# Single row blocks as seven half products, side by side in the array

## The chip, the cores and the metric

One core of a Trainium2 chip. The metric is the device time of one execution in microseconds. Before the change three runs gave 1431.31 to 1433.48, median 1432.56. The engines are named as in the profile: PE is TensorE (PEld its weight loads), DVE VectorE, ACT ScalarE, POOL GpSimd, SP SyncE, whose queue issues DMAs.

## What is computed

Batch 8, 4224 tokens, 192 channels. First a causal convolution of 7 taps over the tokens, with one softmax of taps per head of 24 channels; its result is `x` below. Then:

```python
theta = x @ w_theta
zr, zi = x * cos(theta), x * sin(theta)
y = einsum('ts,bsd->btd', w_tok_r, zr) + einsum('ts,bsd->btd', w_tok_i, zi)
u = x + y
out = u + maximum(u @ w_ch, 0)
```

The two products with the 4224 x 4224 token matrices are nearly all of the work.

## The kernel before, in words

The 4224 tokens are 33 **chunks** of 128 source tokens (four stretches of 32 from four quarters of the sequence), and 33 **row blocks** of 128 output tokens. A chunk is loaded (`load_chunk`), convolved (`conv`, L212), transposed, multiplied with `w_theta` (`theta`), and leaves in SBUF its values `z`: cosine and sine parts for two halves of the columns, Z11, Z12, Z21, Z22, and sums of these, T1 to T4 (`sums`, L303; the combinations of a Strassen-Winograd scheme). It holds a place among 11 for 17 steps.

A **step** (class `Step`, L343) multiplies the 11 chunks then in SBUF (fewer near the ends of a round) with the weights of two row blocks, a pair; 17 steps make a round, and there are 58 steps, 0 to 57. As 33 is odd, one step in each round has a single row block: steps 6, 23, 40 and 57. Steps 6 and 23 have all 11 chunks and are not among the last.

In a pair step the 2 x 2 blocks (two row blocks by cosine and sine weights "11", "12", "21", "22"; two halves of the 1536 columns) are done with seven products instead of eight. `load_w` (L376) loads one of the two weight matrices for the step by four POOL DMAs into a tile `st` (two buffers); `turn` (L394) transposes a part of it in blocks of 32x32 on DVE into a tile `wt` (nine buffers); `wsum` (L402) makes the sums S1 to S4. `w_tasks` (L414) and `early_tasks` say when. These transposed parts and sums are called the step's forms. `runs` (L492) lists the seven runs, each over all chunks, 2 x 11 matmuls of 128x384; `give` (L482) then adds a finished accumulator of 128x768 (PSUM) into the row block's partial sums `pv` in SBUF: on DVE, but on ACT as a copy where it is the first visit in the first round. Such an addition or copy is called an eviction. A single step has four runs without the scheme (11·Z11, 11·T1, 12·Z21, 12·Z22 with two accumulators): 88 matmuls, four times 22, and four evictions.

The accumulators are tiles of two PSUM banks; `ypool` has two (tag "y") and `mmpool` two (tag "mm", `banks`), the latter used otherwise for convolution, transposes and channel products. A run that opens on a reused accumulator must wait until its eviction has read it.

Order: each engine's own work is issued in an order written out by hand (`pe`, `dve`, `act`, `pool`, L85 to L95 chain each instruction to the one before on its engine). `step_events` (L719) collects for each step tasks with a place from 0 to 7 (sevenths of the step's matmuls); `mix` (L587) issues those that are due ahead of each matmul. So a DVE task stands in DVE's queue between the evictions of the runs around its place, and an instruction that waits there holds all that are behind it. DMAs of the SP queue are placed by the framework's scheduler.

Partial sums go to DRAM (`part`) at a step's end and come back one round later (`load_rows`). Into some of the second round's row blocks the convolution's result is added: `load_x` (L457) loads the rows into `xr` (one buffer) by the SP queue, `add_x` (L465) adds them on POOL, not before the DVE instruction issued just ahead of it has ended (`paced`). The first such blocks are the two of step 24, so their additions lie in step 23.

Of the kernel before, what the change touches and what calls it, by code (L numbers as in the profile page):

```python
# [9 lines left out]
AT = mybir.ActivationFunctionType  # L10
ALU = mybir.AluOpType
F16 = mybir.dt.float16
# [4 lines left out]
def kernel(  # L17
# [23 lines left out]
    nc = tc.nc  # L41
# [3 lines left out]
    P = nc.NUM_PARTITIONS  # L45
    assert (B, D, P) == (8, 192, 128) and S % P == 0
    N = B * D
    HD = D // 2
    HN = N // 2
    NQ = 4  # L50
    Q = P // NQ
# [7 lines left out]
    BH = HN // 2  # L59
    NU = (NT + 1) // 2  # L60
    NW = 11
# [5 lines left out]
    start = [base[k % NW] + (NU + 1) * (k // NW) for k in range(NK)]  # L67
# [17 lines left out]
    def pe(ins):  # L85
        return in_order("pe", ins)

    def dve(ins):
        return in_order("dve", ins)

    def act(ins):
        return in_order("act", ins)
# [11 lines left out]
    wpool = ctx.enter_context(tc.tile_pool(name="wpool", bufs=2))  # L104
# [10 lines left out]
    part = [dram.tile([NT, P, N], F32, name=f"part{i}") for i in range(2)]  # L115

    def banks(name, dtype=F32):
        return mmpool.tile([P, 2, PC if dtype == F32 else 2 * PC], dtype,
                           name=name, tag="mm")
# [11 lines left out]
    def loose(name, dtype=F32):  # L131
        return ypool.tile([P, 2, PC if dtype == F32 else 2 * PC], dtype,
                          name=name, tag="y")
# [50 lines left out]
    Z11, T1, Z21, Z22, T2, T4, T3 = range(7)  # L184
    Z12 = T3

    class Chunk:
# [120 lines left out]
        def sum(self, o, a, b):  # L308
            z = self.z
            dve(nc.vector.tensor_tensor(  # L310
                out=z[:, o, :], in0=z[:, a, :], in1=z[:, b, :], op=ALU.subtract
            ))
# [30 lines left out]
    class Step:  # L343


        def __init__(self, t):
            self.t, self.u, self.ks = t, unit(t), active(t)
            self.n = len(self.ks)
            self.tbs = [tb for tb in (2 * self.u, 2 * self.u + 1) if tb < NT]
            self.pair = len(self.tbs) == 2  # L350
            self.first = t < NU
            self.final = t + NU >= NSTEP
            self.late = self.final and self.n < NW
            visits = [v for v in range(NU, NSTEP) if v % NU == t % NU]
            quiet = [v for v in visits if start[2 * NW - 1] < v <= 2 * NU]
            self.adds, self.ahead = [], []
            for i, tb in enumerate(self.tbs):
                known = self.known(tb)
                if t not in ([v for v in quiet if known < v - 1] or visits[-1:])[:1]:
                    continue  # L360
                if not self.late:
                    self.adds.append(i)
                else:
                    far = known <= start[2 * NW - 1]
                    self.ahead.append((i, 2 * NU - NW + 2 * (t % NU) if far else start[-1],
                                       (t // NU - 1 - far) % 2))
            self.plain = self.first and self.pair and self.n <= NP
            self.time = 0.324 * self.n * (8 if self.plain else 7 if self.pair else 5 if self.n <= 2 else 4)
            self.closing = False
            self.st, self.w, self.xr, self.ub, self.uT, self.pv = {}, {}, {}, {}, {}, []  # L370

# [4 lines left out]
        def load_w(self, m):  # L376

            w = (moe_w_tok_r, moe_w_tok_i)[m - 1]
            st = wpool.tile([P, 2, NQ, NW * Q], F16, name="st", tag="st", bufs=2)
            n, nb = self.n * Q, len(self.tbs)  # L380
            for a in range(NQ):
                t0 = token(self.ks[0], a)
                pool(nc.gpsimd.dma_start(  # L383
                    out=st[a * Q : (a + 1) * Q, 0:nb, :, 0:n]
                    .rearrange("i r bt s -> i (r bt) s"),
                    in_=w[self.tbs[0] * P : (self.tbs[0] + nb) * P, t0 : t0 + n]
                    .rearrange("(bt i) s -> i bt s", i=Q),
                ))
            self.st[m] = st
# [4 lines left out]
        def turn(self, name):  # L394
            self.w[name] = self.wtile()
            dve(nc.vector.transpose(  # L396
                self.w[name][:, 0 : self.n, :, :],
                self.st[int(name[1])][:, int(name[0]) - 1, :, 0 : self.n * Q]
                .rearrange("p bt (c j) -> p c bt j", j=Q),
            ))  # L400

        def wsum(self, name):  # L402
            a, b, op = {
                "S1": ("21", "22", ALU.add), "S2": ("S1", "11", ALU.subtract),
                "S3": ("11", "21", ALU.subtract), "S4": ("12", "S2", ALU.subtract),
            }[name]
            self.w[name] = self.wtile()
            dve(nc.vector.tensor_tensor(  # L408
                out=self.w[name][:, 0 : self.n, :, :],
                in0=self.w[a][:, 0 : self.n, :, :],  # L410
                in1=self.w[b][:, 0 : self.n, :, :], op=op,
            ))

        def w_tasks(self):  # L414

            if not self.pair:
                return [(0.25, lambda: self.turn("11")), (4.2, lambda: self.turn("12"))]
            if self.plain:
                return []
            if self.ahead_of_single():  # L420
                return [
                    (0.3, lambda: self.turn("22")), (1.1, lambda: self.wsum("S1")),
                    (1.9, lambda: self.wsum("S2")), (2.9, lambda: self.turn("12")),
                    (4.0, lambda: self.wsum("S4")),
                ]
            return [
                (0.25, lambda: self.turn("11")), (1.2, lambda: self.turn("21")),
                (2.05, lambda: self.wsum("S3")), (2.2, lambda: self.turn("22")),
                (3.05, lambda: self.wsum("S1")), (3.3, lambda: self.wsum("S2")),
                (4.2, lambda: self.turn("12")), (5.1, lambda: self.wsum("S4")),  # L430
            ]

        def ahead_of_single(self):
            return self.final and not steps[self.t - 1].pair and self.pair

        def early_tasks(self):

            return [
                (5.9, lambda: self.turn("11")), (7.0, lambda: self.turn("21")),
                (7.01, lambda: self.wsum("S3")),  # L440
            ]
# [110 lines left out]
        def mix_halves(self, events):  # L552
# [31 lines left out]
            for _, f in events:  # L584
                f()

        def mix(self, events):  # L587

            if self.n <= 2 and not self.first:
                yield from self.mix_halves(events)  # L590
                return
            items = list(self.products())
            events = sorted(events, key=lambda e: e[0])
            y = {}
            for j, (wn, zn, cn, c, opens, closes, to) in enumerate(items):
                if opens:
                    y[cn] = ypool.tile([P, 2, PC], F32, name="y", tag="y")
                while events and events[0][0] * len(items) <= 7 * j:
                    events.pop(0)[1]()
                k = self.ks[c]  # L600
                yield k
                for q in range(2):
                    pe(nc.tensor.matmul(  # L603
                        y[cn][:, q, 0:BH],
                        lhsT=self.w[wn][:, c, :, :].rearrange("p bt i -> p (bt i)"),
                        rhs=chunks[k].z[:, zn, q * BH : (q + 1) * BH],
                        start=opens, stop=closes,
                        skip_group_check=True,
                    ))
                if to:  # L610
                    self.give(y[cn], *to)
            for _, f in events:
                f()
            if not self.final:
                for i, tb in enumerate(self.tbs):
                    nc.sync.dma_start(
                        out=part[(self.t // NU) % 2][tb, :, :], in_=self.pv[i]
                    )

        def cast_half(self, i, h, gs, by_dve):  # L620

# [97 lines left out]
    def step_events(t):  # L719
# [13 lines left out]
        if t + 2 < NSTEP:  # L733
            nxt = steps[t + 2]
            if steps[t + 1].ahead_of_single():
                found.append((4.5, lambda: nxt.load_rows(True)))
            for m in (1, 2):
                at = 1.3 + 3 * (m - 1)
                if steps[t + 1].ahead_of_single():
                    at = (0.1, 3.1)[m - 1]  # L740
                found.append((at, lambda m=m: nxt.load_w(m)))
            if nxt.ahead_of_single():
                found += nxt.early_tasks()
        if t == NPS:
            found.append((5.5, lambda: chunks[EARLY].plain_sums()))
        if t == NPS + 1:
# [241 lines left out]
```

## Time and profile before

| | |
|---|---|
| profiled execution | 1430.95 us |
| its span | 1429.2 us |
| median of three runs | 1432.56 us |
| PE busy | 1408.4 us, 99% |
| DVE busy | 973.2 us, 68% |
| POOL busy | 435.3 us, 30% |
| ACT busy | 312.0 us, 22% |
| granted TensorE clock | 0.999 |
| mixing matmuls (L603) | 7652, 1278.2 us |

The profile shows one execution. A group's row gives the line, the engine, what is written from what, the shape and the count; then its busy time, the mean length of one in ns, and after the bar the idle time of its engine just before, with what ended it. A timeline's row gives start and length in us; instructions in succession are merged, their number at the end. Matmuls overlap in the pipeline: a row of 0.326 us stands for a pitch (start to start) of half that.

### The profile page before, as it was taken

How to read it: one execution, taken by the hardware profiler on the slowest of the kernel's cores; microseconds unless marked ns; L12 is line 12 of the kernel's file. 1: busy time of each engine (PE TensorE's matmuls, PEld its weight loads, DVE VectorE, ACT ScalarE, POOL GpSimd, SP SyncE). 2: the span in 40 equal slices, each digit the busy share in tenths (PEclk: the TensorE clock that was granted, in tenths of full speed). 3: DMA queues.
4: the chain of work that ended last, by engine and by line, in shares of the span. 5: the costliest groups of instructions: out<-in, count | busy, mean ns of one | idle time of the engine just before them, and what ended most of it. 6: DMA issues, size and time to landing. Idle time of an engine off the chain costs nothing.

```text
span 1429.2 us, 23781 instructions
## 1 busy us (share of the span) xinstructions
PE 1408.4 (99%) x9829; PEld 889.5 (62%) x9829; DVE 973.2 (68%) x1047; ACT 312.0 (22%) x377; POOL 435.3 (30%) x655
## 2 busy tenths in 40 slices
PE   8899999999999999999999999999999999999997
PEld 5566666666666666666666666666566666666665
DVE  6884654545458787766665657877777677767686
ACT  5951111011134253000000004435100110010134
POOL 8521221111323322532333343233324123213110
PEclk9999999999999999999999999999999999999999
DMA  9975765564699999898899889999999999999784
GB/s 190 250 174 111 148 146 109 121 134 95 160 227 221 244 217 257 197 262 173 237 229 235 226 157 244 230 200 245 272 206 211 215 210 215 203 200 198 167 219 134
DMA packets 272046, 282.00 MB, mean 197 GB/s; under 512 B 106688, under 2 KB 240192, under 8 KB 271936
## 3 DMA queue, kind: packets, MB, share of 16 engines
q0 software_dynamic: 162464, 92.15, 49.0%
q1 hardware_dynamic: 71840, 178.88, 35.4%
q10 hardware_dynamic: 37632, 9.44, 4.3%
q8 instruction: 77, 1.26, 0.4%
q14 instruction: 33, 0.27, 0.1%
HBM read 245.49 MB, written 108.13 MB: 247 GB/s over the span
## 4 chain that ended last, share of the span: by engine, by line
PE 88%; DMA 5%; DVE 4%; ACT 1%; issue 1%; POOL 1%; SPq 0%; DVEq 0%; ACTq 0%; POOLq 0%
PE y L603 80%; PE v L150 5%; DMA st<-in_moe_w_tok_i_dram 2%; DMA st<-in_moe_w_tok_r_dram 1%; PE tp L174 1%; DMA xw<-in_x_dram 1%; PE pc L220 1%; DVE wt L396 1%; DVE pv L490 1%; ACT z L295 1%; POOL st L383 1%; DVE z L310 0%; DVE z L301 0%; DMA xs<-z 0%; DVE pv L652 0%
## 5 line engine op out<-in xcount | busy, mean ns | idle before, releaser
L603 PE MATMUL y<-z,wt 128*128 128x384 f16 x7652 | 1278.2, 326 | 2.1 <-DVE pv L490 1.0
L603 PEld LDWEIGHTS <-wt 128*128 128x128 f16 x7652 | 741.9, 98 | 477.2 <-issue 3.6
L490 DVE TENSOR_TENSOR pv<-y,pv 128x768 f32<-128x768 f32 x315 | 300.8, 955 | 320.5 <-PE y L603 274.9
L396 DVE STREAM_TRANSPOSE wt<-st 128x1408 f16<-128x1408 f16 (+7 forms) x224 | 327.7, 1466 | 44.2 <-PE y L603 36.2
L383 POOL DMA_DIRECT2D st<-in_moe_w_tok_r_dram x232 | 132.7, 578 | 457.9 <-DVE wt L396 450.9
L383 POOL DMA_DIRECT2D st<-in_moe_w_tok_i_dram x232 | 132.7, 579 | 402.6 <-DVE wt L396 390.3
L408 DVE TENSOR_TENSOR wt<-wt 128x1408 f16<-128x1408 f16 (+6 forms) x208 | 173.6, 835 | 41.8 <-PE y L603 39.4
L160 ACT ACTIVATE z<-pc 128x768 f16<-128x768 f32 (+1 forms) x62 | 47.5, 803 | 385.4 <-PE pc L220 381.1
L160 ACT ACTIVATE ub<-pv 128x768 f16<-128x768 f32 (+1 forms) x66 | 51.5, 821 | 338.7 <-DVE pv L490 336.9
L488 ACT ACTIVATE pv<-y 128x768 f32<-128x768 f32 x66 | 53.7, 814 | 278.5 <-PE y L603 278.5
L150 PEld LDWEIGHTS <-uT 128*128 128x128 f16 x1056 | 90.5, 98 | 22.9 <-issue 5.6
L468 POOL TENSOR_TENSOR pv<-pv,xr 128x1536 f32<-128x1536 f32 x24 | 74.5, 3104 | 66.1 <-issue 26.8
L207 POOL DMA_DIRECT2D xw<-in_x_dram x132 | 76.4, 585 | 28.8 <-DMA st<-in_moe_w_tok_r_dram 7.1
L652 DVE SCALAR_TENSOR_TENSOR pv<-v,pv 128x768 f32<-128x768 f32 (+1 forms) x67 | 63.0, 942 | 25.2 <-PE v L150 24.7
L310 DVE TENSOR_TENSOR z<-z 128x768 f16<-128x768 f16 x132 | 71.2, 553 | 2.3
L295 ACT ACTIVATE z<-v,half_pi 128x768 f16<-128x768 f32 x66 | 59.6, 903 | 56.2 <-PE v L150 55.5
L160 ACT ACTIVATE uT<-tp 128x1536 f16<-128x1536 f16 (+1 forms) x47 | 56.7, 1208 | 47.7 <-PE tp L174 47.7
L301 DVE TENSOR_TENSOR z<-z 128x1536 f16<-128x1536 f16 (+1 forms) x68 | 60.6, 926 | 5.1 <-ACT z L295 5.1
L150 PE MATMUL v<-wth,uT 128*128 128x192 f16 x528 | 54.4, 246 | 2.7 <-ACT z L295 2.1
L150 PE MATMUL v<-wch,uT 128*128 128x192 f16 x528 | 54.4, 246 | 0.8 <-DVE pv L652 0.5
L295 ACT ACTIVATE z<-v 128x768 f16<-128x768 f32 x66 | 53.2, 807 | 0.0
L220 PE MATMUL pc<-xw,bands 96*64 96x192 f16 x512 | 30.1, 250 | 4.1 <-DMA st<-in_moe_w_tok_r_dram 2.2
(48 smaller groups left out, 152.0 us busy)
## 6 DMA issues: line engine op xcount, KB each, us to landing
part<-pv SPq DMA_DIRECT2D x79, 768.0 KB, 4.3
pv<-part SPq DMA_DIRECT2D x79, 768.0 KB, 6.3
out_dram<-pv SPq DMA_DIRECT2D x65, 384.0 KB, 4.3
st<-in_moe_w_tok_r_dram POOLq DMA_DIRECT2D x136, 176.0 KB, 5.9
st<-in_moe_w_tok_i_dram POOLq DMA_DIRECT2D x136, 176.0 KB, 5.2
xs<-z SPq DMA_DIRECT2D x132, 96.0 KB, 5.2
xw<-in_x_dram POOLq DMA_DIRECT2D x121, 96.0 KB, 6.0
xr<-xs SPq DMA_DIRECT2D x24, 384.0 KB, 4.1
```

Of the source, the lines that this page charges most:

```text
L150: pe(nc.tensor.matmul(v[:, k, b * D : (b + 1) * D], lhsT=tT[:, 3 * k + b + i, :], rhs=w[:, 2 * b + i, :], start=(i == 0), stop=(i == 1),))
L160: act(nc.scalar.activation(out=out, in_=in_, func=AT.Copy))
L207: nc.gpsimd.dma_start(out=self.xw[lo : lo + n, h, :, :], in_=x[:, t0 : t0 + n, :].rearrange("b s d -> s b d"),)
L295: act(nc.scalar.activation(**args))
L310: dve(nc.vector.tensor_tensor(out=z[:, o, :], in0=z[:, a, :], in1=z[:, b, :], op=ALU.subtract))
L383: pool(nc.gpsimd.dma_start(out=st[a * Q : (a + 1) * Q, 0:nb, :, 0:n] .rearrange("i r bt s -> i (r bt) s"), in_=w[self.tbs[0] * P : (self.t ...
L396: dve(nc.vector.transpose(self.w[name][:, 0 : self.n, :, :], self.st[int(name[1])][:, int(name[0]) - 1, :, 0 : self.n * Q] .rearrange("p b ...
L408: dve(nc.vector.tensor_tensor(out=self.w[name][:, 0 : self.n, :, :], in0=self.w[a][:, 0 : self.n, :, :], in1=self.w[b][:, 0 : self.n, :, : ...
L468: ins = pool(nc.gpsimd.tensor_tensor(out=self.pv[i], in0=self.pv[i], in1=self.xr[i], op=ALU.add))
L490: dve(nc.vector.tensor_tensor(out=o, in0=yv, in1=o, op=ALU.add))
L603: pe(nc.tensor.matmul(y[cn][:, q, 0:BH], lhsT=self.w[wn][:, c, :, :].rearrange("p bt i -> p (bt i)"), rhs=chunks[k].z[:, zn, q * BH : (q + ...
L652: dve(nc.vector.scalar_tensor_tensor(out=ub[:, ks, :], in0=v[:, ks, :], scalar=0.0, in1=ub[:, ks, :], op0=ALU.max, op1=ALU.add,))
```

## The change

For steps 6 and 23 (`halves`) the single row block is cut into two halves of 64 rows, which take the part of the two row blocks in the seven-product scheme: 11 and 21 are the halves of the transposed cosine weights, 12 and 22 those of the sine weights. Each product has 64 output rows and 384 columns at a time, so two of them are placed side by side in the array, one in its columns 0 to 63 and one in 64 to 127, with accumulators of their own. Four slots: (11·Z11, S1·T1), (S2·T2, S4·Z22), (S3·T3, 12·Z21), and 22·T4 with six chunks on one side and five on the other. Within a slot all chunks are done for one half of the columns, then for the other, and each of the four accumulators is evicted (64 partitions by 384) before the next slot uses it again. The second side's accumulators come from `mmpool`.

The sums S1 to S4 of a single step are four DVE operations of 128 x 704. Both weight matrices of a single step go into one `st` tile, issued together, which leaves the other buffer for the next pair's first matrix, loaded one step earlier than before. The forms of the pair step behind a single step (7 and 24) are made during three steps instead of one: their "11" and "21" (for step 7 also S3, "22" and S1) in the step before the single one, the others within the single step, most of them at its end. The second weight load of the step after that (8 and 25) is moved from place 4.3 to 7.1 of the single step.

In the engines' queues: DVE gets "11" and "21" of step 24 into step 22, where "12" of step 23 stood and behind it; POOL has the two additions `add_x` of step 24 directly behind each other, then the weight load of step 25, which stood between them; SP has the load of `xr` for step 25's first addition ahead of the store of step 23's partial sums.

```diff
+            self.halves = not self.pair and self.n == NW and not self.final
...
         def load_w(self, m):
+            joint = self.halves and m == 2
+            if joint:
+                st = self.st[1]
+            else:
+                st = wpool.tile([P, 2, NQ, NW * Q], F16, name="st", tag="st", bufs=2)
...
+        def half(self, name):
+            tile, i = {
+                "11": ("11", 0), "21": ("11", 1), "12": ("12", 0), "22": ("12", 1),
+                "S1": ("S1", 0), "S2": ("S1", 1), "S3": ("S3", 0), "S4": ("S3", 1),
+            }[name]
+            return self.w[tile][:, :, 2 * i : 2 * i + 2, :]
...
         def w_tasks(self):
+            if self.halves:
+                return [(0.25, lambda: self.turn("11")), (1.2, lambda: self.turn("12")),
+                        (2.2, self.half_sums)]
             if not self.pair:
                 return [(0.25, lambda: self.turn("11")), (4.2, lambda: self.turn("12"))]
+            if self.behind_halves():
+                if steps[self.t - 1].first:
+                    return [(4.0, lambda: self.wsum("S2")), (7.0, lambda: self.turn("12")),
+                            (7.01, lambda: self.wsum("S4"))]
+                return [(3.96, lambda: self.turn("22")), (5.93, lambda: self.wsum("S1")),
+                        (7.0, lambda: self.wsum("S2")), (7.01, lambda: self.turn("12")),
+                        (7.02, lambda: self.wsum("S4")), (7.03, lambda: self.wsum("S3"))]
...
         def early_tasks(self):
+            if self.behind_halves() and not steps[self.t - 1].first:
+                return [(4.6, lambda: self.turn("11")), (5.5, lambda: self.turn("21"))]
+            if self.behind_halves():
+                return [
+                    (4.3, lambda: self.turn("11")), (5.2, lambda: self.turn("21")),
+                    (5.3, lambda: self.wsum("S3")), (6.15, lambda: self.turn("22")),
+                    (6.4, lambda: self.wsum("S1")),
+                ]
...
+        def mix_rows(self, events):
+            n = self.n
+            m = (n + 1) // 2
+            every, fore, back = range(n), range(m), range(m, n)
+            slots = [
+                (("11", Z11, every, True, (0, 0)), ("S1", T1, every, True, (1, 1))),
+                (("S2", T2, every, False, (0, 1)), ("S4", Z22, every, False, (0, 1))),
+                (("S3", T3, every, False, (1, 1)), ("12", Z21, every, True, (0, 0))),
+                (("22", T4, fore, False, (1, 0)), ("22", T4, back, True, (1, 0))),
+            ]
...
+                            if opens and c == 0:
+                                y[q, side] = loose("y") if side == 0 else banks("y")
+                            to = slice(64 * side, 64 * side + 64)
+                            pe(nc.tensor.matmul(
+                                y[q, side][to, q, 0:BH],
+                                lhsT=self.half(wn)[:, cs[c], :, :]
+                                .rearrange("p bt i -> p (bt i)"),
+                                rhs=chunks[self.ks[cs[c]]].z[:, zn, q * BH : (q + 1) * BH],
+                                start=opens and c == 0, stop=c == len(cs) - 1,
+                                skip_group_check=True,
+                            ))
...
+                        if self.first and (q, i, h) not in copied:
+                            copied.add((q, i, h))
+                            act(nc.scalar.activation(out=o, in_=v, func=AT.Copy))
+                        else:
+                            dve(nc.vector.tensor_tensor(out=o, in0=v, in1=o, op=ALU.add))
...
+                if nxt.halves:
+                    at = 1.3
+                if nxt.behind_halves():
+                    if m == 1:
+                        continue
+                    at = 2.3
+                if steps[t + 1].behind_halves() and m == 2:
+                    at = 7.1
                 found.append((at, lambda m=m: nxt.load_w(m)))
...
+            if nxt.halves:
+                found.append((4.4, lambda: steps[t + 3].load_w(1)))
```

## Prediction

> **What bounds the kernel now.** I read the page first (busy shares, chain of waits), then the busy time by stage, then the timelines around the two steps that change.
>
> ```profile
> PE 1408.4 (99%) x9829; PEld 889.5 (62%) x9829; DVE 973.2 (68%) x1047; ACT 312.0 (22%) x377; POOL 435.3 (30%) x655
> ...
> PE 88%; DMA 5%; DVE 4%; ACT 1%; issue 1%; POOL 1%; SPq 0%; DVEq 0%; ACTq 0%; POOLq 0%
> ...
> L603 PE MATMUL y<-z,wt 128*128 128x384 f16 x7652 | 1278.2, 326 | 2.1 <-DVE pv L490 1.0
> ```
>
> TensorE is the bound: in 1429 us its mixing matmuls waited 2.1 us. So a removed matmul is worth its pitch, and every new wait of TensorE costs its full length. Counting mixing matmuls in the trace places the steps: step 6 lies at 146.69 to 160.99, step 22 at 541.78 to 568.01, step 23 at 568.01 to 582.31, step 24 up to 607.34. The stages of 22, 23, 24:
>
> ```profile
> 541.78:568.01 26.23, 26.23 (x216) 17.41 (x214) 17.54 (x23) 12.32 (x14) 4.57 (x8) 1.00 1.01 273
> 568.01:582.31 14.30, 14.30 (x90) 8.61 (x88) 13.07 (x12) 0.00 (x0) 7.21 (x9) 1.00 1.06 293
> 582.31:607.34 25.03, 25.03 (x157) 15.07 (x155) 18.44 (x15) 0.00 (x0) 11.89 (x12) 1.00 0.81 170
> ```
>
> The columns are the stretch, its length, PE, PEld, DVE, ACT and POOL busy (instructions), the granted clock, the DMA share and GB/s. Step 23 is 88 matmuls in 14.30 us, a pitch of 0.1625 with no gap (so is step 6). But DVE is busy 13.07 of those 14.30 us, and the DMA engines are full: the second engine has almost no room here.
>
> **What is removed: 3.25 us.** A single step's 88 matmuls become 78 slots (66 pairs, then 6 per half of the columns). Whether a pair costs one pitch is shown by the convolution, which already places 64-column products side by side:
>
> ```profile
> 410.91 0.81 PE L603 MATMUL y<-z,wt 128*128 128x384 f16 x4
> 411.66 0.85 PE L220 MATMUL pc<-xw,bands 96*64 96x192 f16 x16
> 412.44 0.50 PE L603 MATMUL y<-z,wt 128*128 128x384 f16 x2
> ```
>
> Sixteen such matmuls start within 0.60 us (the 0.85 less the last one's 0.246): eight pairs, 0.0825 us apart after the first, while eight products of 192 columns with whole weights (0.83 us with their last 0.246) start 0.083 apart each. So a pair costs what one costs. Two steps save 2 x 10 x 0.1625 = 3.25.
>
> **Entering and leaving the halves: +0.37.** Around the convolution the gap is 0.254 in and 0.178 out, against 0.1625 and 0.0825: 0.09 extra each way, 0.19 per step (bounds 0 and 0.19; the row is the same event, so I take 0.19).
>
> **More evictions.** Instead of four evictions of 128x768 a step has 16 of 64x384. The nearest row is the 128x384 addition out of PSUM in the last step, 0.553 us, the next one 0.085 before its end (0.035 behind it if it needs its result); ScalarE's 128x384 copy takes 0.49. Fewer partitions could not make it longer; half of it is the lower bound. An eviction starts 0.36 after its last matmul's start (582.15 to 582.51 in the timeline) and TensorE 0.05 after the eviction it waits for. Each of 16 accumulators is reused eleven pairs (1.79 us) later, in the last slot six (0.98).
>
> Step 6: ScalarE makes the first visits, VectorE the rest; each reuse but one is met by 0.3 us or more. The last slot's second half needs two evictions within 0.98 us: 0.36 + 0.47 + 0.553 + 0.05 - 0.16 = 1.27, so **+0.29**. VectorE's added work in step 5 (four half sums of about 0.53, between rows of 0.49 for 640 and 0.55 for 768 elements, three transpositions and two sums for step 7) is 8.7 us in a stage where it was busy 6.84 of 25.03: hidden.
>
> **Step 22's tail and step 23: +1.31.** Here the forms of step 24 are pulled forward into VectorE's fullest place:
>
> ```profile
> 558.12 0.96 DVE L490 TENSOR_TENSOR pv<-y,pv 128x768 f32<-128x768 f32 x1 [0.51 <-PE y L603]
> 558.99 2.20 DVE L310 TENSOR_TENSOR z<-z 128x768 f16<-128x768 f16 x4
> 561.11 1.64 DVE L396 STREAM_TRANSPOSE wt<-st 128x1408 f16<-128x1408 f16 x1
> 562.68 0.92 DVE L490 TENSOR_TENSOR pv<-y,pv 128x768 f32<-128x768 f32 x1
> 563.52 1.81 DVE L301 TENSOR_TENSOR z<-z 128x1536 f16<-128x1536 f16 x2
> 565.24 1.14 DVE L310 TENSOR_TENSOR z<-z 128x768 f16<-128x768 f16 x2
> 566.30 0.95 DVE L490 TENSOR_TENSOR pv<-y,pv 128x768 f32<-128x768 f32 x1
> 567.17 1.14 DVE L310 TENSOR_TENSOR z<-z 128x768 f16<-128x768 f16 x2
> 568.23 0.95 DVE L490 TENSOR_TENSOR pv<-y,pv 128x768 f32<-128x768 f32 x1
> ```
>
> No idle time after 558.12. The change puts step 24's "11" in the place of the transposition at 561.11 and adds "21" behind the eviction of 562.68, so all that follows moves by 1.65. (The half sums and step 23's "12" go to idle places of 3.51 and 2.64 us ahead of the evictions at 553.86 and 549.39.) The eviction of 566.30 frees the accumulator that step 23 opens: it now ends at 568.91, TensorE is ready at 568.10: +0.86. The last one ends at 570.84 and the second accumulator is wanted at 570.76: +0.14. Then VectorE, alone in this step, keeps up until the transposition "22" (1.64) comes between slots 2 and 3; the evictions behind it end at 579.62 and 580.09, and slot 4 wants them at 579.84: +0.31.
>
> **Step 24: +5.10.** Slot 4's evictions end at 583.97, step 24 starts at 582.4 (+0.19 waiting for the first of them). Then VectorE has in this order: S2 (0.89), "12" (1.64), S4, S3, step 25's "11" (1.64), and only then step 24's first eviction, which TensorE needs after two runs of 3.575, at 589.5. Undisturbed it would end at 590.5: +1.05. But a sum that meets GpSimd's addition waits for it:
>
> ```profile
> 577.39 3.10 POOL L468 TENSOR_TENSOR pv<-pv,xr 128x1536 f32<-128x1536 f32 x1 [2.55 <-DVE wt L408]
> 584.71 3.10 POOL L468 TENSOR_TENSOR pv<-pv,xr 128x1536 f32<-128x1536 f32 x1 [1.97 <-DMA xr<-xs]
> 600.62 3.10 POOL L468 TENSOR_TENSOR pv<-pv,xr 128x1536 f32<-128x1536 f32 x1 [9.21 <-issue]
> ```
> ```profile
> 579.81 1.42 DVE L408 TENSOR_TENSOR wt<-wt 128x1408 f16<-128x1408 f16 x1
> ...
> 601.26 3.21 DVE L408 TENSOR_TENSOR wt<-wt 128x1408 f16<-128x1408 f16 x1
> ```
>
> Sums of 0.89 took 1.42 and 3.21, and ended 0.75 after the addition (580.49, 603.72). In the changed order the two additions stand together on POOL. The first is paced by slot 2's eviction (575.81), ends at 579.0, and lets SP load the next rows of x; that load took 3.95 before, so the second addition runs from about 583.3 to 586.4. S2 is ready at 583.9, in its middle, and ends at 587.1. The first eviction of step 24 ends at 592.8: a wait of **3.35** (2.4 to 4.4 for a load of 3.0 to 5.0 us).
>
> Step 25's second weight load, moved from 4.3 to 7.1, now stands behind the second addition and "12" (588.7). Its four DMAs landed 6.8 us after their first issue in a quiet place (563.05 to 569.83), 10.3 in a full one (572.55 to 582.89) and 13.6 at worst (603.67 to 617.24). Here the store of step 23, which SP now issues behind the load for the next addition, at 586.8, and a load of partial sums stand beside it: I take 10.3, landing at 599.0. Transposition "22" waits for it, with step 24's third eviction behind: that ends at 601.55, wanted at 600.04: **+1.56** (0 for 8.7 and less, 4.9 for 13.6). With the 0.19 this is 5.10.
>
> Other moves cost nothing: step 23's two loads share one buffer and go out together, which makes one load of x 2.3 us later (landed 535.4, wanted at 542.2); step 8's late load delays only a transposition with ScalarE's evictions beside it; step 25's sums for x are already loaded.
>
> **Sum.** -3.25 + 0.37 + 0.29 + 1.31 + 5.10 = **+3.82**. The profiled execution took 1430.95 (span 1429.2 and 1.75 around it): 1434.8. It lies 1.6 under the median of the runs, 1432.56; beside the median the forecast is **1436.4**.
>
> **The rivals.**
> (a) VectorE keeps up everywhere: -3.25 + 0.37 = -2.9, 1429.7, faster. For it: VectorE is only 68% busy over the span. Against it: 13.07 of 14.30 in the very step. Chance 0.07.
> (b) Not slower: the addition misses the sums. If the rows of x land later than 4.9 us, or early enough to be done by 583.9, the first wait of step 24 falls to 1.05 and the weight load goes out at 586.4, landing so that the second wait is about 1.5 still: sum +1.5, 1434.1, no difference. For it: the sums and the addition meet only twice in the whole trace. Against it: S2, "12", S4 and S3 fill 4.6 us in a row, and S4 is met when S2 is not. With the cases where waits come out at the low end of their bounds, 0.27.
> (c) The weights, not the products, set the pace of a pair: two loads of 0.110 us (the convolution's 64 columns; 128 columns take 0.098) one behind the other would make 0.22 a pair: 2 x (78 x 0.22 - 14.30) = +5.7, plus 0.37 and 0.86 (the slower step lets VectorE catch up): 1439.5. Against it: the convolution's loads overlap, two within 0.0825. Chance 0.06. [...]
> (d) No pairing at all: 66 more pitches a step, +21.5: 1454.0. Against it the convolution row. Chance 0.03.
> (e) The weight load lands at its worst (13.6): +7.2, 1439.7. Chance 0.09.
>
> **Chances.** The forecast itself has 0.48. A measurement of this kernel tells about 0.2% (2.9 us) from no change. Slower by more: the forecast but for 0.11 of it near the line, and (c), (d), (e): 0.55. Within: (b) and that 0.11, 0.38. Faster: 0.07. The range leaves out (a), (d) and a little at both ends: 1432.0 to 1440.0.
>
> **What would show it.** Right: 154 half matmuls in each single step, pairs 0.1625 apart; TensorE waiting for VectorE's evictions at the start of step 23 (about 0.9) and in step 24 (about 3 and 1.5), a sum of 3 us beside a GpSimd addition just after step 23; step 6 shorter by 1.1. Wrong: pairs further apart, or step 24 still 25.0 us long.

## The result, and the profile after

The changed kernel takes 1438.45 us (median of 16 runs, 1434.03 to 1442.66), the kernel before beside it 1431.57 (16 runs, 1429.81 to 1433.48): a ratio of **1.0042** (95% interval 1.0034 to 1.005), so about 6.0 us slower (the two medians lie 6.9 apart). The forecast was 1436.4. The profiled execution took 1438.38, span 1436.7.

The page of the changed kernel: the busy times, the chain of waits, and the group that stands for L603 of before.

```profile
PE 1411.2 (98%) x9961; PEld 894.0 (62%) x9961; DVE 986.5 (69%) x1075; ACT 314.2 (22%) x383; POOL 434.4 (30%) x655
...
PE 91%; DVE 4%; DMA 3%; ACT 1%; issue 1%; POOL 0%; SPq 0%; DVEq 0%; ACTq 0%
...
L715 PE MATMUL y<-z,wt 128*128 128x384 f16 x7476 | 1252.3, 326 | 7.3 <-DVE pv L542 5.9
```

The whole matmuls waited 2.1 us before and wait 7.3 now, 5.9 of it for VectorE's eviction (L542, L490 before). DVE's busy time rose by 13 us in 1436, one point of its share: the page's averages do not show where it lacks time. Busy time by stage does (steps 23 and 24; columns as in the prediction: the stretch, its length, PE, PEld, DVE, ACT, POOL, the granted clock, DMA share, GB/s).

```profile
571.08:585.12 14.04, 13.38 (x154) 10.68 (x154) 11.43 (x19) 0.00 (x0) 3.11 (x1) 1.00 0.92 281
585.12:615.74 30.62, 26.86 (x154) 15.66 (x154) 23.35 (x21) 0.00 (x0) 16.12 (x15) 0.94 0.74 149
```

Step 23 is 14.04 us (14.30 before) although it issues 78 slots instead of 88 matmuls; step 24 is 30.62 (25.02 before), and the granted clock in it is 0.94. TensorE's timeline across these steps, each line a stretch of matmuls with the idle time ahead of it:

```profile
571.08 11.21 PE L666 MATMUL y<-z,wt 128*64 128x384 f16 x133 [0.66 <-DVE pv L542]
582.56 2.18 PE L666 MATMUL y<-z,wt 128*64 128x384 f16 x21 [0.27 <-DVE pv L685]
585.12 7.31 PE L715 MATMUL y<-z,wt 128*128 128x384 f16 x44 [0.38 <-DVE pv L685]
596.19 4.11 PE L715 MATMUL y<-z,wt 128*128 128x384 f16 x14 [3.76 <-DVE pv L542]
```

Every wait is for an eviction on VectorE, and the large one is 3.76 us ahead of step 24's third run (3.92 by the distance of the two matmuls' starts less a pitch; waits are given that way below). What VectorE did meanwhile:

```profile
584.51 2.32 DVE L685 TENSOR_TENSOR pv<-y,pv 64x384 f32<-64x384 f32 x4
586.87 3.44 DVE L439 TENSOR_TENSOR wt<-wt 128x1408 f16<-128x1408 f16 x1
590.23 1.63 DVE L404 STREAM_TRANSPOSE wt<-st 128x1408 f16<-128x1408 f16 x1
591.90 1.69 DVE L439 TENSOR_TENSOR wt<-wt 128x1408 f16<-128x1408 f16 x2
593.51 1.64 DVE L404 STREAM_TRANSPOSE wt<-st 128x1408 f16<-128x1408 f16 x1
595.18 0.96 DVE L542 TENSOR_TENSOR pv<-y,pv 128x768 f32<-128x768 f32 x1
...
600.69 1.65 DVE L404 STREAM_TRANSPOSE wt<-st 128x1408 f16<-128x1408 f16 x1 [1.37 <-DMA st<-in_moe_w_tok_i_dram]
602.26 0.92 DVE L542 TENSOR_TENSOR pv<-y,pv 128x768 f32<-128x768 f32 x1
```

These are step 23's last four evictions, S2, "12", S4 and S3, step 25's "11", and only then step 24's first eviction, which sets TensorE free at 596.19. S2 took 3.44 us where such a sum takes 0.89, beside this addition on GpSimd, and ended 0.75 after it:

```profile
586.47 3.09 POOL L520 TENSOR_TENSOR pv<-pv,xr 128x1536 f32<-128x1536 f32 x1 [5.28 <-DVE pv L685]
```

The row names an eviction as what released the addition. But its rows of `x`, whose load went out at 581.22, landed only at 586.25, when the eviction that it is paced by had been done for 3.7 us: it waited for `x`.

Then something that the prediction did not have. The stage of 3.41 us that begins 0.46 us after TensorE resumed:

```profile
596.65:600.06 3.41, 3.41 (x13) 1.67 (x11) 2.68 (x3) 0.00 (x0) 2.08 (x4) 0.50 1.23 230
```

The granted clock is 0.50 from end to end, and in it 11 matmuls start, 0.320 us apart, where 21 would at 0.1625: half of the stretch, 1.70 us, is lost with no wait in it.

**Where the time went.** Steps are placed by counting mixing matmuls. Step 6 shows what a pair of half products costs: its 154 half matmuls take 13.15 us, waits included, and the pairs start 0.162 apart, the pitch of one whole matmul.

```profile
150.14 13.15 PE L666 MATMUL y<-z,wt 128*64 128x384 f16 x154
```

After minus before: steps 5 and 6 together -1.13, step 22 +0.83, step 23 -0.26, step 24 +5.60: **+5.04** that belongs to the change. The rest of the 7.5 us between the two spans lies in code that is the same in both: +3.36 before step 4 (waits for rows of `x` in the start-up, with the clock halved once, from 43.69 to 47.11; ten profiles of the kernels below have +0.5 to +2.9 there), -0.12 in steps 41 and 56, -0.80 behind the last mixing matmul.

### The profile page after: what moved, and what is told of

It is laid out like the page before. It is cut to its first block, busy times and chain, and to the rows that moved or that the text cites. A ratio compares the mean times of both kernels' runs of the same rounds, so it can differ in the third digit from the quotient of the medians.

```text
span 1436.7 us, 24086 instructions
## 1 busy us (share of the span) xinstructions
PE 1411.2 (98%) x9961; PEld 894.0 (62%) x9961; DVE 986.5 (69%) x1075; ACT 314.2 (22%) x383; POOL 434.4 (30%) x655
## 4 chain that ended last, share of the span: by engine, by line
PE 91%; DVE 4%; DMA 3%; ACT 1%; issue 1%; POOL 0%; SPq 0%; DVEq 0%; ACTq 0%
PE y L715 80%; PE v L150 5%; DMA xw<-in_x_dram 2%; PE tp L174 2%; PE pc L220 1%; PE y L666 1%; DVE wt L404 1%; DVE pv L542 1%; ACT z L295 1%; DVE wt L439 1%; DMA part<-pv 1%; DVE pv L685 0%; DVE z L310 0%; DVE z L301 0%; DMA st<-in_moe_w_tok_i_dram 0%
## 5 line engine op out<-in xcount | busy, mean ns | idle before, releaser
L715 PE MATMUL y<-z,wt 128*128 128x384 f16 x7476 | 1252.3, 326 | 7.3 <-DVE pv L542 5.9
L715 PEld LDWEIGHTS <-wt 128*128 128x128 f16 x7476 | 725.4, 98 | 472.8 <-issue 11.5
L542 DVE TENSOR_TENSOR pv<-y,pv 128x768 f32<-128x768 f32 x311 | 296.9, 955 | 294.5 <-PE y L715 262.8
L220 PE MATMUL pc<-xw,bands 96*64 96x192 f16 x512 | 30.7, 253 | 3.1 <-DMA xw<-in_x_dram 2.3
```

Of the source, the lines that this page charges most:

```text
L542: dve(nc.vector.tensor_tensor(out=o, in0=yv, in1=o, op=ALU.add))
L715: pe(nc.tensor.matmul(y[cn][:, q, 0:BH], lhsT=self.w[wn][:, c, :, :].rearrange("p bt i -> p (bt i)"), rhs=chunks[k].z[:, zn, q * BH : (q + ...
```

## The experiments

My theory: the halves do save their matmuls; the loss is in step 24, where the forms crowded behind step 23, one of them stopped by a GpSimd addition, hold up the evictions, and the wait then halves the clock. Rivals: the half products cost something of their own; another cause halves the clock; the moved weight load is what holds up step 24.

Each kernel was timed in five rounds beside the kernel before, but for the two with pauses (e5 and e5b), which were run once each. The intervals reach 0.0010 to 0.0017 to either side, 1.4 to 2.4 us, so the small terms are read from the lengths of the steps.

**e1: the halves in step 6 only; e2: in step 23 only.**

```diff
-            self.halves = not self.pair and self.n == NW and not self.final
+            self.halves = not self.pair and self.n == NW and not self.final and self.first      # e1
+            self.halves = not self.pair and self.n == NW and not self.final and not self.first  # e2
```

What was expected of e1:

> Only step 6 is done in halves; step 23 and what surrounds it are as before the change. Theory (the gain of the pairs is real, and all of the loss comes from VectorE's queue around steps 22 to 24): step 6 takes 13.1 us instead of 14.3, steps 22 to 24 as before (26.2, 14.3, 25.0), the time 1.2 us under before (about 1430.4). Rival A (the halves themselves cost, by their loads or by entering and leaving): step 6 not shorter, and half of the loss, some +3 us, stays. Rival B (the start of the kernel got slower with the change): the first 120 us stay 2 us longer in its profile, the time +1.

What was expected of e2:

> Only step 23 is done in halves, with its forms and loads moved as in the change; step 6 is as before. Theory: steps 22 to 24 lose what they lose in the changed kernel (about +0.8, -0.3, +5.6), the time 6 to 7 us over before, that is more than the change as a whole. Rival A: only half of the loss, about +3 us.

e1: 1432.96 (12 runs; before 1431.91, 34 runs), ratio 1.0001 (0.9985 to 1.0017). Step 5 +0.09, step 6 -1.22, nothing at 22 to 24. e2: 1437.55 (12), ratio 1.0033 (1.0019 to 1.0047). Step 22 +0.82, step 23 -0.27, step 24 +6.66. So the whole loss is the second use, and the first one gains the 1.13 that was forecast for it, too little for the medians to tell. e1's profiled execution also had step 38 8.29 longer, a late load of a chunk with the clock halved behind it, in code that the edit does not touch; this is how far apart single executions lie.

Step 24 is 1.06 longer in e2 than in the changed kernel with the same instructions and nearly the same wait (3.85 after 3.92). The stages show why (same columns):

```profile
591.94:595.36 3.42, 0.80 (x5) 0.38 (x4) 3.38 (x4) 0.00 (x0) 2.31 (x4) 1.00 1.04 340
595.36:598.77 3.41, 2.34 (x8) 1.13 (x8) 3.38 (x5) 0.00 (x0) 0.55 (x1) 0.50 1.18 138
598.77:602.18 3.41, 3.41 (x13) 1.51 (x11) 1.93 (x2) 0.00 (x0) 1.74 (x4) 0.50 1.16 321
```

Here the wait (592.58 to 596.43) reaches 1.07 into the first halved stretch, and a second one follows: 6.83 us at half clock instead of 3.41.

**e3: step 24 without its two GpSimd additions.** It leaves out the addition of `x` to step 24's two row blocks, and the loads for it.

```diff
-            for i in steps[t + 1].adds:
+            for i in steps[t + 1].adds if t + 1 != first_add[0] else ():
...
-        if t == start[NW - 1] + 2:
-            found.append((3, lambda: steps[first_add[0]].load_x(first_add[1], True)))
```

What was expected:

> The changed kernel without GpSimd's two additions of the convolution's result into the row blocks of step 24, and without the loads for them (this leaves out that part of the sum for those two row blocks). [...] Rival (the long wait is the row of forms in VectorE's queue alone, whatever GpSimd does): the wait stays above 3 us and step 24 above 29.

1433.71 (12), ratio 1.0013 (0.9996 to 1.003). Steps 6, 22, 23 as in the changed kernel, step 24 **+1.74** instead of +5.60, no half clock. VectorE's timeline, then TensorE's:

```profile
589.18 0.89 DVE L439 TENSOR_TENSOR wt<-wt 128x1408 f16<-128x1408 f16 x1
```

```profile
587.42 7.31 PE L715 MATMUL y<-z,wt 128*128 128x384 f16 x44 [0.38 <-DVE pv L685]
595.95 2.27 PE L715 MATMUL y<-z,wt 128*128 128x384 f16 x13 [1.22 <-DVE pv L542]
```

S2 takes 0.89 again, 2.55 less than beside the addition; the wait at the third run is 1.38 (3.92 less 2.55 is 1.37; 1.05 had been worked out for an undisturbed queue), and a second of 0.37 follows. The addition is thus worth 2.5 us of the first wait. The wait of 3.92 was followed by half clock, those of 1.38 and 0.37 were not.

**e4: step 24's "12", S4 and S3 and step 25's first forms behind step 24's evictions**, with the weight loads of steps 25 and 26 that depend on them.

```diff
-                        (7.0, lambda: self.wsum("S2")), (7.01, lambda: self.turn("12")),
-                        (7.02, lambda: self.wsum("S4")), (7.03, lambda: self.wsum("S3"))]
+                        (7.0, lambda: self.wsum("S2"))]
...
+        def own_tasks(self):                      # issued within step 24
+            return [(1.05, lambda: self.turn("12")), (1.06, lambda: self.wsum("S4")),
+                    (1.07, lambda: steps[self.t + 1].load_w(2)),
+                    (2.05, lambda: self.wsum("S3"))]
...
+                if steps[t + 1].two_behind():     # step 25's forms follow from place 2.06
+                    at = (3.1, 6.1)[m - 1]        # weight loads of step 26
```

What was expected:

> The changed kernel with VectorE's order in step 24 alone changed: S2 is still made ahead of step 24's first eviction, but its 12, S4, S3 and step 25's first forms stand behind the evictions of the first, second and third run, and the weight loads of steps 25 and 26 move with the buffers they need. The additions stay. Theory (the wait is a queue on VectorE in front of that eviction): the eviction ends before TensorE wants it, no wait of 4 us and no halved clock; step 24 takes 25.0 to 26.5, the time within 1 us of before (0 to +1). Rival 1 (the addition that stops S2 is enough by itself): a wait of 1 us or more stays. Rival 2 (the late weight load of step 25 takes the place of the wait): step 24 or 25 wait 1 to 3 us for a transposition that waits for its load.

1438.83 (11), ratio 1.0043 (1.0029 to 1.0058): the second rival. Step 24 is as long as before, with no wait, and step 25 is **6.93 longer**. The second weight load of step 26, issued at 6.1 instead of 4.3, met a GpSimd addition (609.93 to 613.04) and went out at 612.97; it landed at 623.10, 10.1 us after its first issue. VectorE's timeline, then TensorE's:

```profile
623.22 1.65 DVE L404 STREAM_TRANSPOSE wt<-st 128x1408 f16<-128x1408 f16 x1 [6.82 <-DMA st<-in_moe_w_tok_i_dram]
```

```profile
625.76 4.64 PE L729 MATMUL y<-z,wt 128*128 128x384 f16 x14 [4.06 <-DVE pv L556]
```

VectorE stood 6.82 us in front of a transposition whose data was not there, with an eviction queued behind it, TensorE waited 4.2 for that, and the clock was halved for 6.83 us. The cure of step 24 made the same fault one step on.

**e5 and e5b: waits alone.** The kernel before, whole matmuls only, with useless reductions on VectorE ahead of the first eviction of steps 27 to 34.

```diff
+    pause = constp.tile([P, 1], F32, name="pause")
+    DOSE = {27: 6, 28: 7, 29: 8, 30: 8, 31: 9, 32: 9, 33: 10, 34: 11}     # e5
+    DOSE = {27: 7, 28: 8, 29: 9, 30: 10, 31: 9, 32: 8, 33: 10, 34: 12}    # e5b
...
+        if t in DOSE:
+            found += [(0.85, lambda: dve(nc.vector.tensor_reduce(
+                out=pause, in_=wth[:, :, :].rearrange("p a d -> p (a d)"),
+                axis=mybir.AxisListType.X, op=ALU.max
+            )))] * DOSE[t]
```

What was expected of e5:

> The kernel before, whole matmuls everywhere, with a number of useless VectorE reductions (6, 7, 8, 8, 9, 9, 10, 11) ahead of the first eviction of steps 27 to 34, so that TensorE has to wait there: about 1.1, 2.0, 2.9, 2.9, 3.8, 3.8, 4.7 and 5.6 us by my count from the rows of before. After the change TensorE waited 3.92 us in step 24 and the clock record then shows half speed for 3.41 us, which cost 1.7 us beyond the wait. Theory (a wait of TensorE alone brings the halved clock, once it covers a whole window of 3.41 us): none of the waits below 3.4 us is followed by half speed; of the four longer ones some are, 3.41 or 6.83 us each, and each of these makes its step 1.7 or 3.4 us longer than its wait. Rival 1 (a window that is only partly idle is enough): half speed follows waits of 2 to 3 us too. Rival 2 (something else in step 24 of the changed kernel, its DMAs or the 64-column products just before, halves the clock): no wait here is followed by half speed.

What was expected of e5b:

> The same with other counts (7, 8, 9, 10, 9, 8, 10, 12), so that each length of wait comes at another step: about 2.0, 2.9, 3.8, 4.7, 3.8, 2.9, 4.7 and 6.5 us. Theory (the length of the wait decides, against windows of 3.41 us that run on by themselves): none of the three below 3.4 us is followed by half speed; 3.8 seldom, 4.7 sometimes, 6.5 nearly always. Rival 1 (a partly idle window is enough): the 2.9 are, too. Rival 2 (something else in the changed kernel): none is.

The kernels took 1482.15 and 1489.5. A reduction cost 0.99 us in the row, not the 0.90 that I had counted with, so the waits came out longer than expected. TensorE's waits, and the time at half clock that followed, from the traces:

```
e5:   2.25: 3.41   3.24: none   4.23: 3.41   4.23: 3.41   5.22: 6.83   5.22: 3.41   6.20: 6.83   6.93: 6.83
e5b:  3.24: 3.41   4.23: 3.41   5.22: 6.83   6.20: 6.83   5.21: 3.41   4.23: 3.41   6.20: 6.83   7.91: 6.83
```

Fifteen of the sixteen waits were followed by half clock, so nothing peculiar to the changed kernel is needed (the second rival falls). That a whole window must be idle was a supposition of mine, and it falls too, for the first rival: a wait of 2.25 was followed by half clock, while one of 3.24 was not in e5 and was in e5b. The stretches at half clock of one execution begin whole multiples of 3.413 us apart (668.54, 726.57 and 757.29 in e5: 17.0 and 9.0 of them; 43.69 and 596.65 in the changed kernel's profile: 162.0), so I cut time into windows of that length, counted from them. The windows around the waits of 2.25 and 3.24 in e5:

```profile
665.13:668.54 3.41, 1.32 (x9) 0.68 (x7) 3.38 (x4) 0.00 (x0) 0.00 (x0) 1.00 0.47 189
668.54:671.95 3.41, 3.41 (x13) 1.61 (x11) 3.41 (x4) 0.00 (x0) 2.74 (x5) 0.50 0.45 49
692.44:695.85 3.41, 1.84 (x12) 0.98 (x10) 3.27 (x5) 0.00 (x0) 0.00 (x0) 1.00 0.95 362
695.85:699.26 3.41, 1.91 (x12) 1.17 (x12) 3.41 (x4) 0.00 (x0) 0.11 (x1) 1.00 0.21 88
699.26:702.68 3.42, 3.42 (x23) 2.06 (x21) 3.42 (x4) 0.00 (x0) 2.19 (x4) 1.00 0.73 96
```

The shorter wait lies in one window: TensorE idle 2.09 of 3.41, and the next window runs at half clock. The longer one lies across a border: 1.57 and 1.50 idle, and nothing happens. Between step 5 and the last steps, in all twelve traces (before, after and these ten kernels), no window with 1.64 us idle or less was followed by half clock, and each with 1.83 or more was: about half of a window decided. Ahead of step 5, where TensorE's work is of other shapes, the border was less sharp: 1.69 and 1.78 us idle were followed by half clock (e9, e2), 1.94 was not (e5b). In a halved window less sufficed to keep the clock down: between step 5 and the last steps, with 1.07 idle or more in it (e2 above) a second one followed, with 0.21 or less none.

**e6, e7, e9: is there a version that wins?** e6 is e4 with "22" and "12" of step 25 turned one behind the other, so that step 26's load can go at 5.1, ahead of the addition. e7 is e6 with step 24's "21" turned behind step 22's last evictions. e9 is e7 with step 26's "22" behind an eviction.

```diff
-                at = (3.1, 6.1)[m - 1]
+                at = (3.1, 5.1)[m - 1]                                          # e6
-                return [(4.6, lambda: self.turn("11")), (5.5, lambda: self.turn("21"))]
+                return [(4.6, lambda: self.turn("11"))]                         # e7
...
+                return [(0.01, lambda: self.turn("21")), (3.96, lambda: self.turn("22")),
...
-                (2.05, lambda: self.wsum("S3")), (2.2, lambda: self.turn("22")),
+                (2.05, lambda: self.wsum("S3")), (3.04 if late else 2.2, lambda: self.turn("22")),  # e9
```

What was expected of e6:

> Built on e4_order24 (step 24's 12, S4, S3 and step 25's first forms behind the evictions), with one more move: step 25's 22 and 12 are turned one behind the other, so that step 26's second weight load can be issued at place 5.1 of step 24, ahead of the GpSimd addition at 5.6, instead of 6.1. Theory (in e4 that load's late issue, at 612.97 behind the addition, made step 25 6.9 us longer): the load is issued near 605, lands by 616, and step 25 is as long as before, within 0.3 us, with no half speed; step 24 stays as long as before too. What is left of the change is then step 6 -1.2, step 22 +0.8, step 23 -0.3: sum -0.6, a ratio of 0.9996 that cannot be told from no change. Rival (the space of steps 24 and 25 is too tight for the moved forms wherever the load goes): a wait of TensorE of over 1 us appears in step 24, 25 or 26, and the ratio is 1.001 or more.

What was expected of e7:

> e6_earlier_load with step 24's 21 turned at the start of step 23, behind the last evictions of step 22, instead of ahead of them. Theory (the turn ahead of the evictions is what costs step 22 its 0.8 us): step 22 is as long as before within 0.1; step 23's VectorE gets 1.64 us more and has about 13.7 us to do in its 14, so step 23 is between 0.3 us shorter and 0.9 longer than before. Sum with step 6: -1.2 -0.3 to +0.9 = -1.5 to -0.3. Rival (VectorE is the bound of step 23, so that work moved within it only moves the wait): step 23 grows by the 0.8 that step 22 loses or by more, and step 24 begins with the wait: no gain on e6.

What was expected of e9:

> e7_later_21 with one more move: step 26's 22 is turned behind the eviction at place 3 of step 25 instead of ahead of it at 2.2. Theory (step 25's 0.9 us in e6 and e7 is the third eviction queued on VectorE behind that turn, which waits for a weight load that took 15 us): step 25 is within 0.2 us of before, everything else as in e7; what is left of the change's own steps is 6 (-1.2), 22 (+0.1), 23 (-0.4), 25 (0): -1.5 us, ratio 0.999, not to be told from no change by the medians, but by the lengths of the steps. Rival (the turn's lateness only moves): S1 of step 26 comes late for its run and a wait of 0.8 us or more appears in step 25 or 26.

e6: 1432.92 (12; before 1432.66, 23), ratio 1.0005 (0.9995 to 1.0015). The 6.93 us of step 25 are down to 0.83, which is half a miss: the load went out at 605.58, as expected, but landed at 620.67, 15.1 us after its first issue, not by 616, and the third eviction behind the transposition was late by 0.84. e7: 1432.11 (12), ratio 1.0005 (0.9991 to 1.0018). Step 22 +0.09 instead of +0.82, and step 23 -0.37, no longer than in e6: the place of "21" ahead of the evictions was the whole price of step 22, and VectorE has room for it in step 23. Step 25 is 0.91 longer there, much as in e6. e9: 1433.03 (12; before 1432.51, 23), ratio 0.9998 (0.9985 to 1.0011). Step 25 as before; steps 5, 6 and 23 together -1.51. Step 22 was 1.74 longer in the profiled execution, but there the convolution's matmuls (L220) waited 1.38 for rows of `x` from a DMA, not for an eviction; step 18 was 3.72 longer after such a wait, with the clock halved behind it. None of the three can be told from the kernel before by the medians. By the lengths of the steps, with the waits of steps 22, 24 and 25 mended, the change is worth at most 1.5 us of 1431, a tenth of a per cent. The waits of VectorE's evictions at the end of step 23 (0.43, 0.17 and 0.54) are still there in e9; what they would give is not tried.

**e8: the changed kernel with TensorE kept at work during the wait**, by 22 useless matmuls ahead of step 24's third run.

```diff
+                if j == 2 * self.n and self.behind_halves() and not steps[self.t - 1].first:
+                    spare = banks("spare")
+                    for _ in range(22):
+                        pe(nc.tensor.matmul(
+                            spare[:, 0, 0:BH],
+                            lhsT=self.w["11"][:, 0, :, :].rearrange("p bt i -> p (bt i)"),
+                            rhs=chunks[k].z[:, Z11, 0:BH], start=True, stop=True,
+                        ))
```

What was expected:

> The changed kernel with 22 useless matmuls (3.58 us at the pitch of 0.1625, into an accumulator that step 24 doesn't use) ahead of step 24's third run, where TensorE waits 3.92 us for the eviction. The wait on VectorE stays as it is; TensorE has work in it. Theory (the halved clock of 3.41 us, 1.7 us of the 5.6 that step 24 is longer by, comes from TensorE's idle time in one window, and nothing is behind it): no half speed after step 24's wait, step 24 is 3.9 us longer than before (3.7 to 4.2), the kernel 1.7 us faster than the changed one, a ratio of 1.003 against before. Rival 1 (the halved clock has another cause in step 24): half speed for 3.41 us as before, step 24 +5.6 or more, 1.0042. Rival 2 (the second wait of the prediction, for step 25's weight load, lies hidden behind the halved clock): no half speed, but a new wait of TensorE for an eviction of about 1 to 1.6 us later in step 24, which is again 5 to 5.5 us longer than before.

1436.49 (11), ratio 1.0032 (1.0023 to 1.0042). No half clock in step 24, and step 24 is +3.92 instead of +5.60. That is the theory's number, but made up differently: in this execution the addition met S2 1.4 us earlier, S2 took 2.00, and the first eviction was done at 593.41, so that the third run, held by the useless matmuls until 594.55, could have gone after a wait of 2.5. VectorE's timeline, then TensorE's:

```profile
599.51 1.65 DVE L404 STREAM_TRANSPOSE wt<-st 128x1408 f16<-128x1408 f16 x1 [2.92 <-DMA st<-in_moe_w_tok_i_dram]
```

```profile
602.05 4.22 PE L723 MATMUL y<-z,wt 128*128 128x384 f16 x25 [0.19 <-DVE pv L542]
```

A second wait of 0.36 for the weight load's eviction came behind. Without the useless matmuls the fifth run would have been ready at 593.46 + 7.15 = 600.61 and would have waited until 602.05, 1.44 us: the second rival was right that this wait exists, and wrong on its size here, since the filling had used up most of it. The two waits add to 3.9 either way, because the weight load sets the later end. In this execution the wait alone would have left TensorE idle for 1.82 us of one window (589.54 to 592.96 by the trace's half-clock stretches), between the 1.64 and the 1.83 above. So it might not have halved the clock, and e8 supports the 1.7 us and does not prove it; the windows of e5 and the 0.50 stage above carry that.

## Why the prediction was right, and where it was not

The direction, the place and the mechanism held: slower, by step 24's evictions behind forms and a stopped sum. The sum was +3.82; the change's own steps measure +5.04. That the sum comes so near is in part luck: 1.56 us of it, the second wait, did not come, and 1.68 us that it did not have, the halved clock, came in its place. Term by term:

| step | predicted | measured |
|---|---|---|
| 5 and 6: slots saved, entering and leaving, last evictions | -1.14 | -1.13 |
| 22: "11" and "21" ahead of its evictions | +0.86 | +0.83 |
| 23, up to step 24's first matmul | -0.80 | -0.26 |
| 24, first wait | +3.35 | +3.92 |
| 24, second wait, for step 25's weights | +1.56 | 0 |
| 24, clock halved behind the wait | none | +1.68 |

- **What a pair costs** held. Step 6 issues its 154 half matmuls in 13.15 us with the waits in it (the row above), and rival (c), two weight loads setting the pace, would have made it 17.2. Weights of 64 columns did not slow the step, although their loads took 0.110 each and those of 128 columns 0.098: the pairs start 0.162 apart. Rivals (a) and (d) fall with steps 24 and 6. The price of (d) was added wrongly: 66 pitches more than 78 slots are 56 more than the 88 matmuls of before, +18.2 and not +21.5.
- **Step 23** failed in a size. I took 0.47 for the second of two evictions in a row; four in a row take 2.32 with their gaps, 0.59 each (line at 584.51). Waits of 0.11, 0.43, 0.17 and 0.54 (the last in front of step 24) came instead of 0.14, 0.31 and 0.19. On VectorE an eviction of 64 partitions took 0.556 us (mean of the 24 at L685) where the row of before had 0.553 for 128; the half that I had put as the lower bound was not reached.
- **The first wait of step 24** held as a mechanism. The addition began 1.35 us after step 24's start, not 0.9 (583.3 against 582.4), as the load of its rows of `x` took 5.03 us and not 3.95; the wait came out 0.57 longer. S2 took 3.44 us beside the addition and 0.89 in e3 without it; by what the one holds up the other, no run here shows.
- **The second wait** was mis-sized. The load landed 8.4 us after its first issue, where I took 10.3 and had put 0 for 8.7 and less. The eviction behind it was done at 603.23. At full clock the fifth run would have wanted it at 596.19 + 7.15 = 603.34, 0.11 later; with the third run at half clock it came 1.7 later still. So the second wait hid behind the longer first one; in e8 it is there.
- **The step of the prediction that was missing** is the price of a long wait: "every new wait of TensorE costs its full length" is too little. A wait of 3.92 cost 5.60. Rival (b), the addition missing the sums, was not met in any profile but e3's, where the addition is left out; its +1.5 for the sum compares with +1.16 there. The 4.6 us that it gives S2, "12", S4 and S3 in a row are 4.1 in e3 (589.18 to 593.27).

What stays open: by the interval of the ratio the change costs 4.9 to 7.2 us, by the profiled execution's own steps 5.04 and by e2's step 24 one more. With nearly the same wait two windows were halved in e2 (3.85) and one in the changed kernel's profile (3.92), where the wait lay otherwise against them, one case each; how the 16 runs divide is not known.

## What to carry to other kernels

Before counting the matmuls that a change saves, look at what its evictions and forms add on the engine that shares the stage: here 3.25 us of saved slots were paid for in a step where VectorE had 1.2 us free, and the mended versions kept 1.5 at most, by the lengths of their steps. Price a new wait of TensorE by its length, and where about half of a 3.41 us window goes idle, add what the halved clock cost here, 1.6 to 2.8 us (the range over e2, the changed kernel, e5 and e5b). A late form is not cured by moving it behind the eviction unless the load that its buffer feeds still goes out in time: e4 moved 5.6 us of step 24 to 6.9 in step 25.

## What the runs showed of the hardware that was not expected

The granted clock fell to 0.50 after much shorter waits than I had thought: in e5 2.09 us idle within one window of 3.41 was enough, 3.07 idle split over two was not. The stretches at half clock, 3.41 and 6.83 us long, lie on a grid of 3.413. I had supposed one whole window idle to be the condition; what was measured is a share of a window, between 1.64 and 1.83 us idle from step 5 on.

In step 6 the two products of a pair use all 128 rows, and their two loads of 0.110 did not lengthen the pitch of 0.162. The step's 154 loads add up to 16.9 us, and PEld is busy for 8.75 of its 13.10:

```profile
150.00:163.10 13.10, 13.00 (x156) 8.75 (x154) 4.77 (x9) 4.20 (x8) 0.00 (x0) 1.00 0.52 149
```

So the loads overlapped one another, as those of the convolution's pairs had; by what means, no run here shows.

Weight loads of the same size (four DMAs of 176 KB) landed 8.4 (changed kernel, for step 25), 10.1 (e4) and 15.1 us (e6, both for step 26) after their first issue; a plan that is tight by one microsecond against such a load, as those of e4 and e6 were, is decided by that spread.
